# Scalings of K and Q features on GpSimd instead of VectorE, and another order of work, in a linear-attention and gated-MLP block

## Chip, cores and metric

The kernel runs on one core of one Trainium2 chip, in one launch. The metric is the device time of that launch in microseconds (us), the median of several runs; lower is better. A profiled execution gives the times of single instructions.

## What is computed

S = 2048 tokens of width D = 640, one batch, bfloat16. A linear attention with 32 heads of 20 channels is followed by a bilinear MLP with 1536 hidden channels. Cut from the reference:

```
h  = x + A(layernorm(x));  out = h + B(layernorm(h))
A: q, k, v = split(x @ wqkv)                     # 32 heads x 20
   phi(u)  = concat(softmax(u @ w_phi), softmax(-(u @ w_phi)))   # 40 features per head
   kv = sum_s phi(k)_s v_s^T ;  z = sum_s phi(k)_s
   o  = (phi(q) @ kv) / (phi(q) . z + 1e-6) ;  A = o @ wo
B: ((x @ w_gate) * (x @ w_up)) @ w_down
```

## The kernel before

The tokens are 16 tiles of 128 (number t below). Every step is a named operation with an engine, what it reads and writes, and slots in small pools of buffers. The names, with the engine that runs them and the line where they are recorded:

- **Start.** x0 to x14, wk, wv, wq, w5 and the other w are loads by DMA, most of them issued by SyncE (SP). warm are matmuls on zeros. WT transposes the K weights on TensorE and F1, F0 fold w_phi into the K and Q weights; WTe and Fe copy the results out of PSUM.
- **Layernorm.** L1s, L1a (VectorE statistics), L1l, L1e (ScalarE: the reciprocal root by logarithm and exponential), L1n (line 440, a 128x1 product on GpSimd or VectorE) and xn (the normalised tile, VectorE or ScalarE, line 446); xt transposes it into xnT by DMA, or on TensorE for tiles 0 and 1.
- **K and V.** V and K are projections, ten matmuls of 320 columns each; in tiles 0 and 1 each is cut in five parts. Ve copies V out of PSUM (line 510). Kx (two instructions, exp of +u and -u) writes the K features ek, Ks sums each head's 20 on VectorE (line 495), Kr and Ke form the reciprocal on ScalarE, and **Kn** multiplies the features by it (line 515, a tensor_tensor of 128x1280). KV (line 523) adds the tile's kv and z in PSUM. KVe copies the sums out once all 16 are there.
- **Q.** Q, Qx, Qs (line 553), Qr go the same way; **Qb** (line 560) subtracts the two logarithms of a head, Qe takes the exponential, and **Qn** (line 567, tensor_tensor of 128x660) scales the second half of the features. qT transposes them by DMA.
- **Attention output.** N (line 585) multiplies by kv, dd, rd and o divide, oT is a DMA transpose, O (line 612) the output projection, h adds the residual.
- **MLP.** hc centres the tile (ScalarE, or VectorE), hT transposes it by DMA, L2q, L2v (line 633), L2r form the second layernorm's scale; U is a gate or up projection (line 655), g and u form the product, D the down projection (line 674), y scales and adds, w stores.

Tokens of the MLP go in five blocks of 2, 4, 4, 4 and 2 tiles (U0 to U4). PSUM has eight banks; a projection holds two.

The order is neither that of the code nor decided on the chip. PLAN, a table at the top of the file, holds for each operation a due time, the number of the engine chosen from a short list, and the buffer slots. Each engine's program is its operations sorted by due time, and an engine runs its program strictly in order. An operation that waits for a semaphore holds everything behind it on its engine; SP's transposes and loads stand in one such queue. The due times serve for sorting only. The lines that read the table (lines 172 and 173), and the choice that Kn has (lines 515 and 519):

```
k, a, o.slots = PLAN.get(name, (key, 0, ()))
o.eng, o.occ, o.lat = o.alts[a]
...
G.op("pool", "Kn%d" % t, lambda e, eng, ek=ek, sr=sr: e.tensor_tensor(
...
    pool_c(1280), LP, [ek, sr], [ek], kk, alts=[("dve", dve_c(1280), LD)])
```

"pool" is GpSimd, "dve" VectorE; without a number in the table the first of the list is taken. All of this comes before the attention output: KV14 and KV15 need Kn14 and Kn15, and no N can run before KVe0 and KVe1.

Of the kernel before, what the change touches and what calls it, by code (L numbers as in the profile page):

```python
# [49 lines left out]
gl0:0.78 gla2:0.942 gla3:1.084 glb3:1.313 gla1:1.452 gla0:1.594 glb2:1.736 zero:0.91 w5:0.78 Ph1:2.585 x0:0.78 L1s0:3.188 warm0:1.239 warm1:1.665 id0:2.977  # L50
id1:3.216 warm2:2.091 warm3:2.517 x1:1.26 warm4:2.943 warm5:3.369 warm6:3.795 L1a0:4.098 wk0:1.74:1 eps:3.459 L1l0:4.331 L1s1:4.207 L1a1:5.117 warm7:4.221
warm8:4.647::0 warm9:5.077 L1e0:4.657 xn0:5.226::0 L1l1:5.35 L1e1:5.676 xn1:5.914::1 WT0:5.292::1 WTe0:5.912 warm10:5.709 warm11:5.924 warm12:6.139 xt0:6.354::0
xt1:6.633::2 xte0:6.832 glb0:3.49 gla4:3.628 xte1:7.415 x3:2.22:1 L1s3:6.426 L1a3:7.336 wk1:2.7 WT1:6.912::3 WTe1:7.532 L1l3:8 L1e3:8.325 glb1:3.771 Ph0:3.999
wk3:3.18 glb4:4.593 Ph2:4.822 F1_0:7.329::4 Fe1_0:8.418:1 wk4:3.66:1 WT4:7.648::6 WT3:8.065::7 wk2:4.14:1 WT2:8.482::1 WTe2:9.101 ekz:5.415 F1_1:8.899::2
Fe1_1:9.687 WTe4:8.268:1 F1_4:9.218::4 WTe3:8.684 F1_3:9.537::6 F1_2:9.863::0 x2:4.62 L1s2:9.092 K0_0:10.447::2 L1a2:10.002 Fe1_4:10.271:1 K0_1:10.719
L1n3:8.605 xn3:10.111::2 Fe1_3:10.623:1 K1_0:11.031::4 K1_1:11.303 wv0:5.1:1 V1_0:11.573::6 Fe1_2:10.854:1 K1_2:11.845 x4:5.58 L1s4:11.364 L1a4:12.274
K1_3:12.116 K1_4:12.386 K0_2:12.658 K0_3:12.928 x6:6.06 L1s7:12.383 L1s5:13.169 L1l2:11.438 L1e2:11.764 L1n2:12.044 xn2:12.347:1:3 wv4:6.54:1 Kx1_0:13.152::0
Kx1_1:13.736 L1a5:14.079 L1l4:14.319 L1e4:14.646 L1s6:14.188 x14:7.02 wv1:7.5 V1_1:13.2 L1n5:14.976:1 xn5:15.13::0 wv2:7.98:1 V1_2:13.47 L1a6:15.642 K0_4:13.742
Kx0_0:14.739::1 Kx0_1:15.322 L1n4:15.751:1 xn4:15.906:1:1 V0_0:14.012::0 V0_1:14.284 va1:12.268 L1a7:15.796 L1l6:16.712 wv3:8.46 V1_3:14.555 V0_2:14.825
V0_3:15.097 xt3:10.736 x8:12.046 Ks0:16.058::0 V0_4:15.367 V3:15.639::4 Ve3:17.195::0 V1_4:16.994 Ve1:17.779::1 wqt1:12.527 Kr0:18.363 Ke0:18.654 Kn0:18.988  # L60
K3:17.265::2 Kx3_0:18.822::2 x10:13.836 phz:21.3 xt2:14.316 K2:18.622::4 L1s9:17.451 Kx3_1:19.405 L1a9:18.361 xt5:15.755 Ks1:18.471::1 Kr1:19.989 Ke1:20.28
L1s8:19.863 L1a8:20.773 L1e6:20.427 L1n6:20.883:1 L1n7:20.927:1 xt4:17.064 xn7:21.081::2 Kx2_0:20.52::3 wqt4:18.375 wg4:19.684 L1l8:21.104 L1e8:21.43
L1n9:21.668:1 wqt2:20.165 V2:19.977::6 K5:21.334::2 Ve2:21.534::2 Ve0:22.117::3 K4:22.689::6 Kx5_0:22.89::4 Sz:22.017 Kx5_1:23.474 L1s10:21.712 L1n8:22.195
xt7:21.706 Kx2_1:24.058 KV0:24.046::0,1 Ks3:22.5::2 Kr3:24.642 Ke3:24.933 mk0:22.419 V4:24.378::2 Ve4:25.934::4 V5:25.735::4 xn6:23.892::3 L1a10:24.404
x12:23.017 Ks2:24.794::3 xn9:26.186::0 Kx4_0:26.518::1 xn8:26.698::1 Ve5:27.291:1:5 Kx4_1:27.102 Kn1:22.48 KV1:27.09 Ks4:28.021::0 Kn3:25.267 L1s11:29.415
Ks5:30.201::1 L1a11:31.595 Kr2:27.686 Ke2:27.977 K7:27.424::2 wqt3:23.497 Kx7_0:28.98::0 Kx7_1:29.564 Kn2:28.311 V7:28.779::6 Ve7:30.335::6 L1s15:31.703
L1a15:32.614 L1s14:32.722 L1a14:33.633 wqt0:24.806 F0_0:30.136::4 Fe0_0:30.919 Kr5:31.713 L1l10:31.86 L1e10:32.185 L1n11:32.465 xt6:26.116 V6:30.454::2
xt9:27.427 Ve6:32.279::7 xt8:28.736 F0_3:31.811::6 Fe0_3:32.862 wo2:30.047 KV2:32.13 K6:32.462::4 Kr4:33.447 Ke4:33.737 Kn4:34.072 F0_2:33.819::2 Ke5:33.883
Kx6_0:34.029::3 Kx6_1:34.614 xn11:33.742::2 xt11:34.367 Fe0_2:35.197 L1s12:34.254 wu1:35.676 KV3:34.138 K9:34.471::6 wg0:36.157 Kn5:36.385 Kx9_0:36.026::2
Kx9_1:36.611 V8:35.827::4 L1s13:35.041 L1a13:35.95 Ve8:37.383::3 L1a12:36.059 L1l12:37.967 L1e12:38.292 Ks7:36.169::2 rqz:38.697 L1n15:38.734 F0_4:37.182::2  # L70
Fe0_4:38.386 L1n12:38.959 L1n10:37.562:1 xn10:38.969:1:3 Ks9:37.606::3 Kr9:39.775 KV4:37.502 F0_1:37.834::6 Fe0_1:38.999:1 K8:38.154::4 Kx8_0:39.92::1 KV5:39.51
Kx8_1:40.505 K11:39.843::2 Kx11_0:41.398::4 Kx11_1:41.983 Q0_0:41.199::6 Q0_1:41.471 xt10:39.913 Q3:41.742::4 xn15:39.739::0 xt15:41.222 wo0:42.532
Ks6:40.252::0 Kr6:42.566 Ke6:42.858 Q0_2:43.109 Q0_3:43.382 Q0_4:43.654 wg2:43.013 L1n13:41.645:1 xn13:41.798::1 xt13:43.492 L1n14:39.182 Kn6:43.191 Ke9:43.004
Ks8:42.31::1 wg1:44.803 Q1_0:43.925::2 Qx3_0:43.307::0 Qx3_1:43.917 Kr7:44.528 wu0:45.282 Ke7:44.819 Kn7:45.505 Qs3:44.712 Kr8:44.965 Q1_1:44.197
Qx0_0:45.111::1 Qx0_1:45.721 Q1_2:44.469 Q1_3:44.742 Q1_4:45.014 Qx1_0:46.331::2 Qx1_1:46.941 mk1:47.818 Ke8:47.55 Kn8:48.088 xn14:46.148::2 Q9:45.285::4
Qx9_0:47.697::3 Qx9_1:48.306 V10:46.653::6 Ve10:48.916::1 KV6:48.008 K10:48.342::2 Kn9:50.401 Kx10_0:49.898::3 Qs0:46.66 Kx10_1:50.481 KV7:49.697 xn12:48.094::3
K13:50.031::4 Kx13_0:51.587::0 Qr3:52.17::0 Kx13_1:52.316 Q2:51.386::6 Qx2_0:52.952::4 xt12:48.719 xt14:50.029 mk2:52.714 Ks11:48.606::0 Qr0:53.562::1
Qb3:52.984 Qb0:53.906 Qx2_1:53.708 Qs9:49.999 Qr9:54.318::2 Qb9:54.661 Ks10:51.434::2 Kr10:54.464 wd2:51.34 Ke10:54.755 Qe3:54.901 V9:52.754::2 Ve9:55.02::2
Qn3:55.208 Ks13:53.053::1 wd3:51.819 Q5:54.109::4 Qx5_0:55.675::5 V12:55.477::6 Kr13:56.285 Kr11:56.431 qT3:56.542::0 Qe9:56.577 Qs1:54.446 KV8:56.833
KV9:57.166 Ke13:56.696 Qs2:55.88 Qr1:56.842::3 Qe0:56.987 Qn0:57.316:1 Qb1:57.185 Ke11:57.106 Qe1:57.461 Qn1:57.767 qT1:59.102::1 Qn9:59.032 Qr2:57.58::0  # L80
Qb2:58.166:1 Qx5_1:57.725 Qe2:58.38 Qn2:60.297 K12:57.498::2 Kx12_0:59.054::1 Kx12_1:59.639 Ve12:58.266:1:0 K15:58.855::4 Kx15_0:60.41::2 Kx15_1:60.995
wu3:61.578:1 Kn10:58.996:1 Q4:60.211::6 Qx4_0:62.059::0 Qx4_1:62.669 Q10:61.578::2 Ks15:61.73::3 KV10:62.944 Kr15:63.279 Ke15:63.569 Ks12:63.123::2 Kn13:61.562
Qs4:64.516 Qx10_0:63.715::2 Qx10_1:64.326 Qs10:65.951 qT2:61.633::2 K14:63.278::4 qT9:63.123::3 wd0:66.028 Kx14_0:64.936::3 Kx14_1:65.519 qT0:66.508::4
Kr12:66.103 Ke12:66.394 Qr4:66.54::1 Qb4:67.386:1 Ks14:67.487::1 Qs5:68.879 wu2:68.209 V11:64.633::6 Kn15:63.904 Ve11:66.686::4 Q13:65.99::2 Qe4:67.602
Qn4:70.314:1 qT4:71.293::5 wu4:72.782 Qx13_0:67.721::4 Qx13_1:68.331 Qs13:71.165 V13:67.356::4 Kn11:66.216 Kr14:68.999 Ke14:69.29 V14:68.713::6 Ve14:70.269::5
Ve13:70.853::7 Kn12:68.529 Qr10:71.436::3 Q6:70.069::2 Qx6_0:71.633::3 Qx6_1:72.243 Qs6:73.038 Kn14:70.843 V15:71.436::6 Ve15:72.992::6 KV11:72.791 KV12:73.124
KV13:73.457 KV14:73.79 KV15:74.124 Q7:74.457::4 KVe0:74.654 Qr5:73.576::2 Qb5:73.919 Qe5:74.195 Qn5:74.501 Qr13:74.314::0 Qx7_0:76.022::1 Qb13:75.766
Qe13:76.632 wg3:73.263 Qn13:76.939 Qx7_1:76.751 KVe1:75.243 N0:75.823::2 qT5:76.347::4 dd0:76.355::0 rd0:76.57 N2:76.156::6 dd2:76.853::1 o0:76.972::0
oT0:77.9::0 Q11:76.49::0 Qx11_0:78.055::0 Qx11_1:78.665 rd2:77.784 o2:78.186::1 N1:77.856::4 dd1:78.998::0 rd1:79.213 o1:79.615::2 qT13:79.21::2 Q8:78.189::2
N3:79.556::6 Qx8_0:80.558::5 Qx8_1:81.168 dd3:80.427::0 Qs7:80.532 Qr7:82.085::1 Qb7:82.43 rd3:81.968 o3:82.371::0 oT1:80.7::1 N9:79.889::0 dd9:83.181::0  # L90
Q14:80.572::4 O0:81.984::2 Qe7:82.704 Q12:83.343::6 Qx14_0:83.419::4 Qx14_1:84.029 h0:83.541 rd9:84.341 oT2:82.01::2 o9:84.745::2 Qb10:82.629 Qe10:84.639
N4:84.71::2 dd4:85.555::0 rd4:85.77 O1:85.043::4 o4:86.174::1 Qn7:83.011 h1:86.984 O2:86.4::0 h2:87.957 N5:87.758::2 dd5:88.757::0 rd5:88.972 oT3:83.32::3
O3:88.091::4 Qr6:84.758::2 hc0:84.904::0 o5:89.376::0 qT7:84.629::1 hc1:87.919::1 hc2:88.892::3 h3:90.186 Q15:89.45::0 Qs14:90.987 oT9:86.12::0 O9:90.817::2
# [822 lines left out]
```

## Time and profile before

| what | before |
|---|---|
| median of 3 runs | 276.71 us (275.79 to 277.2) |
| profiled execution, whole | 273.92 us |
| its span on the core | 272.2 us |
| TensorE busy in the span | 265.4 us |
| VectorE / ScalarE / GpSimd busy | 169.1 / 125.6 / 66.4 us |
| Kn on GpSimd: 15, mean | 2399 ns |
| Kn on VectorE: 1 | 1908 ns |
| Qn on GpSimd: 12, mean | 1428 ns |
| Qn on VectorE: 4, mean | 1250 ns |
| granted TensorE clock | 1.00 |

Lines of the profile name engines PE (TensorE matmuls), PEld (its weight loads), DVE (VectorE), ACT (ScalarE), POOL (GpSimd) and SPq (SyncE's queue, which issues DMAs). L515 is line 515 of the kernel. In the page's second part each digit is the busy share, in tenths, of one of 40 equal slices of the span, 6.8 us each. In the chain, columns are start, length and what ran; in the timeline they are start, length, engine, line, operation, tile written and tiles read, count, and in brackets the engine's idle time before it with what ended it. Operations can be told apart in the timeline since each engine runs its program in the written order.

### The profile page before, as it was taken

The numbers are of one execution on the slowest core, as the hardware profiler recorded it, in microseconds if no ns is written. First come the engines' busy times: TensorE is split into PE (matmuls) and PEld (weight loads), VectorE is DVE, ScalarE is ACT, GpSimd is POOL, SyncE is SP. The second block draws the span as 40 slices with busy tenths as digits, with TensorE's granted clock in tenths as the row PEclk, the third lists the DMA queues.
The fourth block names the chain that finished last, engine by engine and source line by source line (L and its number), as shares of the span: only waits on it lengthen the run. The fifth ranks groups of instructions, "written<-read, shape, count | busy, mean of one in ns | idle before, by whom it ended". The sixth has DMA issues, their size and how long they took to land.

```text
span 272.2 us, 5184 instructions
## 1 busy us (share of the span) xinstructions
PE 265.4 (97%) x2096; PEld 176.5 (65%) x2096; DVE 169.1 (62%) x304; ACT 125.6 (46%) x309; POOL 66.4 (24%) x88
## 2 busy tenths in 40 slices
...
DVE  5999998999989979587835435313332511434332
ACT  4998899989846565632332223530031210404000
POOL 6229476879954033001100000000000000000000
...
## 3 DMA queue, kind: packets, MB, share of 16 engines
...
q14 instruction: 8, 0.07, 0.1%
...
## 4 chain that ended last, share of the span: by engine, by line
PE 85%; POOL 7%; ACT 3%; DVE 3%; DMA 2%; issue 0%; DVEq 0%
PE ps L655 37%; PE ps L674 19%; PE ps L479 16%; PE ps L612 7%; POOL ek L515 4%; POOL ph L567 2%; DMA Wp<-o 2%; PE ps L585 1%; DVE o L602 1%; PE ps L364 1%; PE ps L523 1%; PE ps L408 1%; ACT ph L548 1%; DVE sm L599 1%; ACT ek L491 0%; ACT xnT L247 0%
## 5 line engine op out<-in xcount | busy, mean ns | idle before, releaser
L655 PE MATMUL ps<-xnT,Wgu 128*128 128x512 bf16 (+1 forms) x600 | 108.0, 336 | 0.0
L655 PEld LDWEIGHTS ps<-xnT,Wgu 128*128 128x128 bf16 x600 | 58.0, 98 | 43.0 <-DVE ev L663 0.2
L660 ACT ACTIVATE gt<-ps 128x512 bf16<-128x512 f32 (+1 forms) x60 | 29.6, 509 | 98.0 <-PE ps L655 86.5
L479 PE MATMUL ps<-Wp,xnT 128*128 128x320 bf16 (+1 forms) x480 | 68.5, 299 | 0.2 <-DVE o L602 0.2
L663 DVE TENSOR_TENSOR ev<-ps,gt 128x512 bf16<-128x512 f32 (+1 forms) x60 | 33.2, 579 | 43.4 <-ACT gt L660 20.8
L479 PEld LDWEIGHTS ps<-Wp,xnT 128*128 128x128 bf16 x480 | 45.2, 97 | 18.6 <-DVE o L602 0.6
L674 PE MATMUL ps<-Wd,ev 128*128 128x320 bf16 (+2 forms) x396 | 53.8, 295 | 0.0
L674 PEld LDWEIGHTS ps<-Wd,ev 128*128 128x128 bf16 x396 | 38.1, 98 | 15.6
L686 DVE SCALAR_TENSOR_TENSOR Wp<-ps,rs,x_all 128x640 bf16<-128x640 f32 (+3 forms) x18 | 14.6, 810 | 39.7 <-PE ps L674 39.5
L515 POOL TENSOR_TENSOR ek<-ek,SR 128x1280 bf16<-128x1280 bf16 x15 | 35.7, 2399 | 11.9 <-ACT SR L500 11.9
L633 POOL TENSOR_SCALAR ln<-mv 128x1 f32<-128x1 f32 x10 | 1.9, 190 | 111.1 <-ACT ek L629 110.8
L612 PE MATMUL ps<-Wo,Wp 128*128 128x320 bf16 x160 | 24.2, 299 | 0.9 <-DMA Wp<-o 0.9
L553 DVE TENSOR_REDUCE S<-ph 128x66 f32<-128x1320 bf16 x16 | 24.1, 1519 | 1.0 <-ACT ph L550 1.0
L495 DVE TENSOR_REDUCE SR<-ek 128x64 f32<-128x1280 bf16 x16 | 23.5, 1472 | 0.4 <-ACT ek L491 0.2
L548 ACT ACTIVATE ph<-ps 128x600 bf16<-128x600 f32 x32 | 21.2, 678 | 3.8 <-PE ps L479 2.3
L491 ACT ACTIVATE ek<-ps 128x640 bf16<-128x640 f32 x32 | 20.7, 700 | 1.5 <-PE ps L479 1.3
L612 PEld LDWEIGHTS ps<-Wo,Wp 128*128 128x128 bf16 x160 | 15.4, 98 | 7.0 <-DMA Wp<-o 1.2
L567 POOL TENSOR_TENSOR ph<-ph,RQ 128x660 bf16<-128x660 bf16 x12 | 17.1, 1428 | 10.9 <-ACT RQ L563 10.7
L618 DVE SCALAR_TENSOR_TENSOR x_all<-ps,x_all 128x640 bf16<-128x640 f32 x16 | 13.1, 821 | 7.7 <-PE ps L612 7.4
L629 ACT ACTIVATE ek<-x_all,mv 128x640 bf16<-128x640 bf16 x16 | 13.1, 820 | 4.7 <-DVE x_all L618 4.7
L602 DVE TENSOR_TENSOR o<-ps,sm 128x720 bf16<-128x720 f32 x16 | 14.5, 906 | 0.8
L560 POOL TENSOR_TENSOR RQ<-RQ 128x32 f32<-128x32 f32 x14 | 3.3, 238 | 29.4 <-ACT RQ L556 29.4
...
## 6 DMA issues: line engine op xcount, KB each, us to landing
...
```

Of the source, the lines that this page charges most:

```text
L479: ins = e.matmul(pb(b, hb)[:, 0:n1 - n0], lhsT=T["xnT"][:, NC - 1 - c, P * t:P * (t + 1)], rhs=T["Wp"][:, POS[kind], c, n0:n1], start=(c = ...
L491: G.op("act", "%sx%d_%d" % (nm, t, s), lambda e, s=s, b=b, ek=ek: e.activation(out=T["ek"][:, ek.slots[0], 0:2 * D].rearrange("p (b h s f) ...
L495: G.op("dve", "%ss%d" % (nm, t), lambda e, ek=ek, sr=sr: e.tensor_reduce(out=T["SR"][:, sr.slots[0], 0, :], in_=T["ek"][:, ek.slots[0], 0: ...
L515: G.op("pool", "Kn%d" % t, lambda e, eng, ek=ek, sr=sr: e.tensor_tensor(out=T["ek"][:, ek.slots[0], 0:2 * D].rearrange("p (h f) -> p h f", ...
L548: e.activation(out=v[:, 0:10].rearrange("p (b g) j f -> p b g j f", b=2), in_=pp(b, 0, 300).rearrange("p b (g j f) -> p b g j f", j=3, f=D ...
L553: G.op("dve", "Qs%d" % t, lambda e, t=t, ph=ph: e.tensor_reduce(out=T["S"][:, t, 0:66].rearrange("p (g k) -> p g k", k=6), in_=pv(ph).rear ...
L567: return e.tensor_tensor(out=v, in0=v, in1=T["RQ"][:, rq.slots[0], 1, 0:33].rearrange("p (g j) -> p g j", j=3).unsqueeze(3).to_broadcast([ ...
L612: ins = e.matmul(pb(b, hb)[:, 0:320], lhsT=T["oT"][:, oT.slots[0], c, :], rhs=T["Wo"][:, c, 320 * hb:320 * (hb + 1)], start=(c == 0), stop ...
L655: ins = e.matmul(pb(b)[:, 0:n], lhsT=T["Wgu"][:, gu, c, P * ft:P * (ft + 1)], rhs=T["xnT"][:, NC - 1 - c, o0:o0 + n], start=(c == 0), stop ...
L660: G.op("act", "g%d_%d" % (bi, ft), lambda e, pg=pg, gt=gt, n=n: e.activation(out=T["gt"][:, gt.slots[0], 0:n], in_=pb(pg)[:, 0:n], func=AF ...
L663: o_ = G.op("dve", "u%d_%d" % (bi, ft), lambda e, pu=pu, gt=gt, hh=hh, ft=ft, n=n: e.tensor_tensor(out=T["hh"][:, hh.slots[0], ft, 0:n], i ...
L674: ins = e.matmul(pb(b, hb)[:, 0:w], lhsT=T["hh"][:, hh.slots[0], ft, P * tt:P * (tt + 1)], rhs=T["Wd"][:, ft, c0 + w * hb:c0 + w * (hb + 1 ...
```

## The change

Only PLAN changes: due times, engine choices and slots, hence each engine's order. No function, operation or shape does. 49 of 1025 operations change engine:

| operations | from | to |
|---|---|---|
| Kn10; Qn0, Qn4, Qn11, Qn12; Qb2, Qb4 | VectorE | GpSimd |
| Qb12 | GpSimd | VectorE |
| L1n4, 5, 6, 7, 9, 10, 13; L2v3, 4, 10, 11, 12 | VectorE | GpSimd |
| L1n3, 8, 11, 15; L2v0, 1, 5, 15 | GpSimd | VectorE |
| Ve4, 11, 13, 14; WTe0; xn2, xn10; hc6, hc7 | ScalarE | VectorE |
| Ve5, Ve12; Fe1_3, Fe0_1; xn6; hc10, 11, 14, 15 | VectorE | ScalarE |
| x1 (issue) | SP | ScalarE |
| w5, wu3 (issue) | ScalarE | SP |

A few entries of the diff (name:due time:engine number:slots):

```diff
-Qb2:58.166:1 Qx5_1:57.725 Qe2:58.38 Qn2:60.297 K12:57.498::2 Kx12_0:59.054::1 Kx12_1:59.639 Ve12:58.266:1:0
...
-wu3:61.578:1 Kn10:58.996:1 Q4:60.211::6
...
+Qb9:54.175 Qe9:54.853 Q2:52.852::2 Kn10:54.431 V9:54.219::4 Qs5:55.515
...
+Qb2:61.609 Ks12:61.829::2
```

The orders that result, where they differ most. GpSimd, from Kn6 to Kn14:

```
before: Kn6 Kn7 mk1 Kn8 Kn9 mk2 Qb3 Qb0 Qb9 Qn3 Qb1 Qn1 Qn9 Qn2 Kn13 Kn15 Kn11 Kn12 Kn14
after:  Kn6 L1n14 L1n13 mk2 L1n12 Kn7 Kn8 Kn9 Kn11 Qb1 Qb0 Qn0 Qn1 Qb9 Kn10 Kn13 Qb3 Qb5 Qn3
        Qb2 Qn2 Kn15 Qn5 Qn9 Kn12 Kn14
```

TensorE, the first projections, and from N7 to N15 (U0_4_1 is block 0, column tile 4, 1 for up):

```
before: F1_1 F1_4 F1_3 F1_2 K0_0 K0_1 K1_0 K1_1 V1_0 K1_2 ...
after:  F1_0 F1_2 F1_4 F1_1 V1_0 V1_1 V1_2 F1_3 V1_3 K1_0 K1_1 ...
before: N7 U0_10_0 U0_0_1 U0_1_1 U0_0_0 U0_5_0 O4 U0_1_0 N10 U0_2_0 U0_3_1 U0_4_1 U0_3_0 U0_2_1 U0_9_0 N6
        U0_4_0 U0_6_1 U0_10_1 U0_5_1 O5 U0_6_0 U0_8_0 O7 O6 U0_7_0 U0_9_1 O10 N15
after:  N7 U0_10_0 U0_2_0 U0_0_0 U0_1_1 U0_9_0 U0_0_1 O4 N10 U0_1_0 U0_2_1 O5 U0_5_0 N6 U0_7_1 U0_4_0
        U0_3_1 U0_3_0 U0_5_1 U0_4_1 U0_8_0 U0_7_0 O7 U0_6_1 U0_6_0 O10 U0_11_0 O6 U0_11_1 N15
```

SP's queue at the start and around oT6:

```
before: x0 x1 wk0 x3 wk1 wk3 wk4 wk2 x2 wv0 x4 x6 wv4 ...   qT6 oT7 hT3 hT2 oT10 wd1 oT6 qT15 hT5 hT4
after:  w5 wk0 x0 wk4 x3 wk3 wk2 wk1 wv0 x4 wv1 wv2 wv3 ... wd3 qT6 oT7 hT3 oT10 hT5 hT2 oT6 qT15 hT4
```

More of the change, by code (lines that the diff above doesn't have):

```diff
@@ L49 @@
 for _t in """
[L50 to L93, printed above, removed]
@@ L102 @@
-Qe11:107.364 oT6:102.826::1 hc4:107.483::1 h7:107.275 qT15:104.136::5 O6:107.075::4 h6:108.632 hT5:106.647 Qn11:109.433:1 hc7:108.21::2 U0_7_0:108.433::1
-L2q0:108.927 g0_8:109.787::2 U0_9_1:108.979::0 g0_7:110.061::3 O10:109.525::6 h10:111.082 N15:110.883::4 hT4:108.338 L2v5:107.55 dd15:111.882::0 rd15:112.097
-o15:112.501::2 U0_7_1:111.216::2 qT14:109.648::4 u0_7:113.311 U0_8_1:111.762::1 u0_8:113.642 hc6:110.335::3 u0_9:113.973 U0_11_0:112.308::6 qT11:111.138::1
-hT7:113.319 oT15:114.629::2 U1_0_0:112.854::7 N13:113.933::4 dd13:114.464::0 rd13:114.679 o13:115.082::1 U1_1_0:114.266::2 g0_11:113.763::3 U1_2_0:115.345::1
@@ L106 @@
-Qs12:115.893 g1_2:116.622::2 U1_5_0:116.424::6 g1_1:117.109::1 L2v2:117.328:1 N14:117.503::4 U1_3_0:117.836::0 Qr12:117.596::2 dd14:118.034::0 rd14:118.249
-o14:118.653::0 U1_9_0:118.915::1 u0_10:119.463 U0_11_1:119.995::2 u0_11:120.739 Qb12:117.94 Qe12:118.215 Qn12:121.07:1 O15:120.54::4 L2q7:118.334 L2v7:119.382
-L2v1:119.549 hT6:115.939 L2v0:119.718 L2v9:119.885 h15:122.097 hc15:123.031:1:0 g1_9:120.192::0 Qs8:123.484 Qr8:125.037::0 Qb8:125.382 Qe8:125.656
-U1_0_1:121.898::3 D0_0:122.978::1 oT14:119.579::3 O14:126.237::4 hc10:124.919:1:1 L2r2:125.373 L2r0:125.442 y0_0:126.436::0 g1_0:125.775::3 hT15:123.606
@@ new lines @@
+L1a1:4.098 L1l1:4.331 wk0:1.26:1 va1:1.708 warm4:2.943 warm5:3.369 warm6:3.795 warm7:4.221 x0:1.74 L1s0:4.207 L1a0:5.117 warm8:4.647::0 warm9:5.077 warm10:5.292
+L1e1:4.657 warm11:5.507 xn1:5.226::0 gla2:2.538 L1l0:5.35 L1e0:5.676 xn0:5.914::1 gla4:2.68 warm12:5.722 id0:2.822 id1:3.061 xt1:5.937::0 wk4:2.22:1 x3:2.7:1
+WT0:6.216::1 WTe0:6.835:1 xt0:6.633::2 wk3:3.18 xte1:6.415 xte0:7.111 L1s3:7.244 wk2:3.66:1 gla1:3.304 wk1:4.14 WT4:6.912::3 WTe4:8.03:1 WT2:7.407::4 L1a3:8.438
+WTe2:8.027 L1l3:8.671 WT3:7.824::5 WTe3:8.547 wv0:4.62:1 WT1:8.241::6 WTe1:8.956 L1e3:8.998 glb4:3.446 Ph2:3.675 L1n3:9.364:1 x4:5.1 xn3:9.648::2 L1s4:10.159
@@ new lines @@
+L1s5:10.947 L1a4:11.733 glb1:4.269 Ph0:4.497 L1a5:11.857 phz:5.091 glb2:5.808 Ph1:6.036 F1_0:8.658::0 Fe1_0:9.175:1 F1_2:8.977::2 wv1:5.58 F1_4:9.296::4
+Fe1_4:9.813:1 ekz:6.428 F1_1:9.615::6 Fe1_1:10.397 Fe1_2:10.981:1 V1_0:9.936::0 rqz:6.662 wv2:6.06:1 V1_1:10.207 V1_2:10.478 F1_3:10.749::4 Fe1_3:11.565
+wv3:6.54 V1_3:11.068 K1_0:11.339::6 K1_1:11.61 x2:7.02 L1s2:11.966 L1a2:12.876 L1l4:12.149 L1e4:12.475 L1n5:12.755 xn5:13.057::3 K0_0:11.881::2 K0_1:12.152
+K0_2:12.423 K0_3:12.694 K0_4:12.965 x6:7.5 L1s7:13.569 L1l2:13.108 L1e2:13.434 L1n2:13.714 xn2:14.356::0 Kx0_0:13.527::0 Kx0_1:14.111 K1_2:13.236 K1_3:13.507
@@ new lines @@
+Kn2:28.623 Kx7_1:31.104 L1n11:32.745:1 x14:22.502 L1s14:32.92 xt6:22.982 V6:29.901::0 wqt3:24.292 Ve6:31.688::7 KV2:31.257 KV3:31.59 L1n10:31.291 Kr4:32.272
+Ke4:32.563 wqt4:25.602 wqt1:26.912 F0_2:31.923::2 Fe0_2:32.709 L1a14:33.83 F0_3:32.242::4 Fe0_3:33.293 L1s15:33.939 K6:32.561::0 Kx6_0:34.117::3 Kx6_1:34.701
+F0_0:33.917::2 wu3:28.222 xn11:34.726::2 Kn5:31.515 Fe0_0:35.285 xt9:29.326 K9:34.236::4 Kx9_0:35.869::2 Kx9_1:36.453 xt8:30.678 V8:35.592::0 Ve8:37.148::1
+L1a12:35.238 Kn4:33.828 wg0:31.988 L1s13:35.347 Ks6:36.134::2 Kr6:37.732 Ke6:38.023 Kn6:38.357 L1a15:37.527 L1a13:37.636 KV4:36.948 L1l12:38.169 xt11:35.351
@@ new lines @@
+L1e12:38.495 L1n14:40.67 Ks7:37.745::0 L1n13:40.894 mk2:41.118 L1n12:41.389 KV5:37.281 F0_4:37.614::2 Fe0_4:38.588 wu1:36.661 F0_1:37.933::4 Fe0_1:39.172
+K8:38.252::0 Kx8_0:39.808::0 Kx8_1:40.392 xn10:39.138::3 Kr7:40.976 Ke7:41.267 Kn7:41.612 K11:39.608::2 Q3:40.964::4 Kx11_0:41.413::4 Kx11_1:41.997
+Q1_0:42.331::0 xt10:39.763 wo2:41.073 Ks9:39.65::3 Q1_1:42.603 Ks8:41.128::1 Q1_2:42.875 Q1_3:43.147 Q1_4:43.419 Q0_0:43.691::2 Qx3_0:42.581::0 Kr8:43.191
+Ke8:43.482 Q0_1:43.963 Q0_2:44.235 Qx3_1:43.628 Kn8:43.925 wu0:41.553 xn12:42.521::0 Q0_3:44.507 Q0_4:44.779 Qx1_0:44.238::1 xn13:43.033::1 Ks11:43.545::2
@@ new lines @@
+Qs9:51.252 Qr9:53.66::2 Kr10:53.806 Ke10:54.097 Qs3:52.687 Qx5_1:54.243 Ks13:54.122::1 Qb9:54.175 Qe9:54.853 Q2:52.852::2 Kn10:54.431 V9:54.219::4 Qs5:55.515
+Ve9:55.775::4 Kr13:56.359 Qx2_0:56.505::5 Ke13:57.115 Kn13:57.449 Qx2_1:57.261 Qr3:57.871::3 V12:55.575::0 Ve12:58.017::3 K15:56.931::4 Kx15_0:58.601::0
+Kx15_1:59.185 Qs2:58.056 Qb3:59.762 KV9:58.287 KV10:58.62 Ks15:59.921::3 Qr5:59.769::1 Qb5:60.113 wu2:56.651 Qe3:60.037 Qn3:60.344 K12:58.953::2 Qr2:60.156::0
+Q4:60.309::0 Kx12_0:60.509::2 Kx12_1:61.093 Qe5:61.677 V14:61.676::4 Qb2:61.609 Ks12:61.829::2 qT3:61.679::2 wg1:63.169 Ve14:63.232:1:6 Qe2:61.884 Qn2:62.191
@@ new lines @@
+Kr15:62.003 Ke15:62.294 Kn15:63.456 Kr12:63.341 Qx4_0:63.487::2 Qx4_1:64.097 Qs4:64.892 Q10:63.032::2 Qx10_0:64.707::1 qT2:63.649::3 Qx10_1:65.317 Qs10:66.327
+Qn5:65.769 wo0:65.349 Qr4:66.445::3 K14:64.399::4 V13:65.755::0 Ve13:67.762:1:2 Ke12:66.591 Kx14_0:66.737::3 Kx14_1:67.321 Ks14:68.493::0 Q13:67.111::2
+Qx13_0:68.676::0 Qx13_1:69.286 V11:68.478::4 Ve11:70.034:1:7 Q6:69.834::0 KV11:71.201 Kr14:70.005 Ke14:70.296 Qs13:70.765 Qn9:67.034 qT9:68.369::4 Kn12:68.299
+Qx6_0:71.399::5 Qx6_1:72.009 Qs6:72.804 V15:71.534::2 qT5:69.859::5 KV12:72.89 KV13:73.223 Ve15:73.09::5 Kn14:70.63 KV14:73.556 KV15:73.889 KVe0:74.42
@@ new lines @@
+KVe1:75.009 Q7:74.222::4 Qb4:72.943 Qe4:73.674 Qn4:73.981 N0:75.589::0 dd0:76.12::0 rd0:76.335 wg4:72.039 N1:75.922::2 Qr13:73.793::0 dd1:76.625::1
+Qx7_0:75.787::3 Q11:76.255::6 Qb13:75.246 qT4:76.113::0 o0:76.749::0 Qe13:76.397 Qn13:76.704 N2:77.705::0 oT0:77.676::0 rd1:77.56 Qx7_1:76.516 Qx11_0:77.82::4
+Qx11_1:78.43 Q8:78.038::4 Qx8_0:80.323::2 qT13:78.986::1 o1:77.974::1 N3:79.405::2 Q14:79.738::6 dd2:78.785::0 rd2:79 oT1:80.476::1 Qx8_1:80.933 o2:79.414::2
+oT2:81.786::2 N9:81.105::0 dd3:80.225::0 O0:81.75::4 Qs7:80.331 Qr7:81.884::1 rd3:81.766 o3:82.18::0 oT3:83.107::3 h0:83.307 dd9:84.127::0 rd9:84.342
```

104 lines of the change are left out of this document (64 added, 40 removed).

## The prediction

> **What bounds the kernel now.** I read the page's busy shares first, then its slices, the chain that ended last, and the timeline around the two longest stops of TensorE.
>
> ```profile
> span 272.2 us, 5184 instructions
> ...
> PE 265.4 (97%) x2096; PEld 176.5 (65%) x2096; DVE 169.1 (62%) x304; ACT 125.6 (46%) x309; POOL 66.4 (24%) x88
> ...
> DVE  5999998999989979587835435313332511434332
> ACT  4998899989846565632332223530031210404000
> POOL 6229476879954033001100000000000000000000
> ```
>
> TensorE is busy for 265.4 of 272.2 us. Both kernels run the same matmuls, so whatever an order can win lies in the other 6.8 us: about 1.3 us of start, 2.7 us behind the last matmul, and 2.9 us of stops between. Up to slice 11 (75 us) VectorE is as full as TensorE and ScalarE nearly so; GpSimd fills up at the end of that stretch. There a late feature can stop TensorE. After 112 us the chain is TensorE alone. The chain of waits names two places:
>
> ```profile
> 58.02 5.31 POOL ph L567 x3
> 63.33 12.24 POOL ek L515 x5
> 75.56 0.05 issue
> 75.61 0.85 PE ps L523 x22
> ...
> 105.50 4.59 DMA Wp<-o
> 110.09 0.05 issue
> 110.14 1.53 PE ps L612 x10
> ```
>
> First place: KV14 waits for Kn14, the end of 17.5 us of unbroken GpSimd work. The timeline by engine shows why that work was long:
>
> ```profile
> 58.02 5.31 POOL L567 TENSOR_TENSOR ph<-ph,RQ 128x660 bf16<-128x660 bf16 x3 [0.34 <-ACT RQ L563]
> ...
> 60.26 1.91 DVE L515 TENSOR_TENSOR ek<-ek,SR 128x1280 bf16<-128x1280 bf16 x1
> ...
> 70.86 2.48 DVE L567 TENSOR_TENSOR ph<-ph,RQ 128x660 bf16<-128x660 bf16 x1
> ...
> 75.61 0.85 PE L523 MATMUL ps<-ev,ek 128*128 128x63 bf16 x22 [1.39 <-POOL ek L515]
> ...
> 110.14 0.31 PE L612 MATMUL ps<-Wo,Wp 128*128 128x320 bf16 x1 [0.88 <-DMA Wp<-o]
> ```
>
> A Qn alone takes 1.30 us on GpSimd (ten of the twelve), a Kn 2.36. The three Qn from 58.02 took 5.31 instead of 3.9, and Kn14 took 2.95, while VectorE ran its own Kn10 and Qn4. Qn4 took 2.48 on VectorE where the three Qn that meet no GpSimd work take 0.84; a Qb there took 1.29 against 0.18. So the two engines' two-input operations waited for each other: GpSimd lost 1.2 (Qn2), 0.2 (Qn1) and 0.6 (Kn14), 2.0 us ahead of KV14. The wait of 1.39 is less than that. Second place: O6 waits 0.88 us for oT6, issued at 105.50 just behind the 480 KB weight load wd1 and landing 4.6 us later, where the median for that transpose is 2.7.
>
> **The scalings moved.** Kn10, Qn0, Qn4, Qn11, Qn12, Qb2 and Qb4 go from VectorE to GpSimd, Qb12 the other way. VectorE sheds 1.9 + 0.8 + 2.5 + 0.8 + 0.8 + 1.3 + 0.2 = 8.3 us, 6.7 of it ahead of KVe0. GpSimd gains 2.36 + 4 x 1.30 + 2 x 0.24 - 0.24 = 7.8 us. Only Qb12 is left on VectorE with two SBUF inputs, at about 123 us when GpSimd is nearly empty, so I price the mutual blocking at nothing: 2.0 us come back to GpSimd. The order also puts Qn5 and Qb5 ahead of Kn14, so ahead of KV14 GpSimd has Kn10, Qn0, Qn5, Qb2 and Qb5 more and the 2.0 less: 2.36 + 2 x 1.30 + 2 x 0.24 - 2.0 = 3.4 us; some L1n add 0.8.
>
> [...]
>
> **Does GpSimd still finish before TensorE needs KV14?** Ahead of KV14 both orders give TensorE the same projections, folds and KV steps, so it arrives at 74.22 us plus what the start slips. GpSimd from Kn7 to Kn14 has nine Kn, six Qn and six Qb: 21.2 + 7.8 + 1.4 = 30.4, less 0.04 of overlap at each step = 29.7 us. When can Kn7 begin? Now GpSimd idles 3.73 us before Kn6 (43.30), since Ks6 stands at 40.23 on VectorE and Kr6 behind the Kx8 and Kx11 pairs on ScalarE. In the new order Ks6 stands ahead of Ks7 and Kr6 directly behind Ve8, which ended at 38.17. That lets Kn6 start near 38.9, and Kn7 (Ke7 behind Kx8, near 42.1) near 42.3 instead of 45.6. Walked step by step with the rows' durations, waits for Kr13 (0.7, behind Ve9), Qe5 and Qe2 (0.9 in all) and others leave 1.9 us of idle time on GpSimd: 42.3 + 29.7 + 1.9 = 73.9, ahead of TensorE by 0.3 to 0.8. The stop of 1.39 goes: **-1.4**. If the cover is gone, each us of lateness costs one us.
>
> **The other moves ahead of KVe0.** VectorE takes Ve4, Ve11, Ve13, Ve14 (0.8 each), xn2, xn10 and WTe0, and gives up Ve5, Ve12, Fe1_3, Fe0_1 and xn6. Of its own L1n it hands over seven and takes four. With the scalings it has about 6 us less to do (11.9 given up, 5.6 taken), ScalarE about 1.6 less. Ve14, Ve13 and Ve11 free PSUM pairs: by the walk they end 0.3 to 1.3 us before their next users. All three sit behind a 1.4 us reduction; lying tight, they are priced at zero but keep up to 0.5 for the range.
>
> **Start.** SP issues w5 and wk0 ahead of x0, which goes at 1.72 us instead of 0.80; x1 goes by ScalarE's queue. The first normalised tiles come some 0.3 us later. On VectorE the copies WTe0, WTe4, WTe3, WTe1 follow with L1s3 between, so the last ends near 9.8 and F1_1 follows; V1_0 to V1_3 then stand ahead of K1_0, and each needs its wv load (issued about 4.5 to 6.4, median 4.9 to landing, so 9.4 to 11.3). When V1_3 has ended (11.7) the old order is 0.3 us further. I take **+0.4**; ends -0.2 (the old stop of 0.3 before F1_4 goes, nothing new) and +1.2 (the last wv late).
>
> **77 to 112 us.** oT, hT and qT transposes pass SP's queue one by one, 1.3 us each. The new order puts O5 early and O10 and three U ahead of O6; oT6 is issued behind hT2, near 105.2, and TensorE asks for O6 near 110.5. Even 4.6 us to landing is in time: **-0.9**. wd1 goes behind qT11, wd0 behind oT15, with nothing urgent next. But wd3 now goes just ahead of qT6 (near 95.1): with 4 to 5.9 us to landing N6 would wait 0 to 0.6. Q12 now takes the banks of N3 and so waits for o3 near 84.2, 0.4 us, where now Q14 waits 0.23 for o1. O5, U0_4_0 and O15 follow their releasers by 0.1 to 0.3. Together **+0.5** (bounds 0 and 1.5).
>
> **112 us to the end.** The L2v swaps (0.14 against 0.19), hc6, hc7, hc10, hc11, hc14, hc15 (0.54 on VectorE, 0.83 on ScalarE) lie on engines under half full, beside a TensorE that never stops there. hT13 and hT12, last before U3_8_0, have some 4 us to spare. Zero; a new stop could cost up to 0.5. The last six D groups keep their length.
>
> **Sum.** -1.4 + 0.4 - 0.9 + 0.5 = -1.4. The profiled execution took 273.92 us (span 272.2 and 1.7 around it), so 272.5. The median shown, 276.71, lies 1.0% above that execution, with runs of 275.79 to 277.2; I put the difference on the median: **275.3 us**.
>
> **Rivals.**
> 1. Only one stop goes. GpSimd is in time, but the 0.9 us comes back as waits behind wd3 and o3, or O6 is late again. For it: SP's queue stays as full. Then -0.5: 276.2.
> 2. Slower: GpSimd becomes the bound. The point is Kn7's start plus idle time: 29.7 us must fit before about 74.6. If Ke7 stays as late as now (Kn7 at 45.6) and the idle is the 2.6 us that GpSimd has today from 53 to 58, Kn14 ends at 77.9: a wait of 3.3 in place of 1.39, +1.9. With the start at +0.4 and the second place unchanged, 279.0. It decides once start delay and idle time exceed 2.6 us together against my 1.9. For: more work there. Against: VectorE, which paced Ks, has 6 us less.
> 3. The start slips by its upper end and only KV14's stop is won, with the tight PSUM handovers taking 1.0: 1.2 - 1.4 + 1.0 = +0.8, 277.5.
> That the change does less than said is excluded by the order listing: Kn and Qn stand on GpSimd all 32 times.
>
> **How the numbers follow.** A measurement of this kernel can tell about 0.5%, 1.4 us, from no change, and my forecast lies on that edge. Forecast 0.47 (0.40 beyond the edge: with the start at -0.2 or the 77 us stretch at 0 it gives 274.7), rival 1 0.24 (0.05 beyond, since runs spread 0.3%), rival 2 0.18, rival 3 0.11 (0.07 past the upper edge). Faster 0.45, same 0.07 + 0.19 + 0.04 = 0.30, slower 0.25. Winning all 2.9 us gives 273.8; below stands little. The upper end takes in most of rival 2: 273.6 to 278.8.
>
> **What would show it.** Right: KV14 directly behind KV13; every Kn near 2.36 and every Qn near 1.30 on GpSimd; Kn7 starting near 42 and Kn14 ending before 74.7; O6 without a wait on its transpose; TensorE busy near 265 in a span near 270.8. Wrong: a wait of L523 or L479 on GpSimd's ek over 1 us (rival 2), first projections past 11.0 us (rival 3), N6 or O waiting on scratch or Wp (rival 1).

## The result: 1.0% faster, and the profile after

The changed kernel took 273.22 us (median of 4 runs, 272.96 to 274.77) where the kernel before took 276.4 (4 runs, 275.79 to 277.2): a ratio of 0.9895, 95% interval 0.9849 to 0.9941. A second comparison on another occasion gave 273.46 (273.35 to 273.73) against 276.11, ratio 0.9902 (0.9879 to 0.9926). The gain is 2.7 to 3.2 us; 1.4 was forecast, and the time lies under the range of 273.6 to 278.8.

The profiled execution took 273.25 us (span 271.5), so on the profiles alone (273.92 before) the gain would be 0.7. This contradiction is the main subject of what follows. The page of the changed kernel:

```profile
span 271.5 us, 5179 instructions
...
PE 266.3 (98%) x2096; PEld 178.0 (66%) x2096; DVE 160.3 (59%) x294; ACT 125.4 (46%) x309; POOL 72.7 (27%) x98
...
DVE  4898999887988899774555643314324221414342
ACT  3799799988766475373135322106312230021100
POOL 8028769989952232204000000000000000000000
...
L515 POOL TENSOR_TENSOR ek<-ek,SR 128x1280 bf16<-128x1280 bf16 x16 | 37.5, 2356 | 4.4 <-ACT SR L500 4.4
L567 POOL TENSOR_TENSOR ph<-ph,RQ 128x660 bf16<-128x660 bf16 x16 | 20.8, 1306 | 11.9 <-ACT RQ L563 11.9
```

VectorE lost 8.8 us and GpSimd gained 6.3. All 16 Kn (L515) now take 2.36 us on average, all 16 Qn (L567) 1.31: nothing is blocked any more. The chain of waits of the changed kernel, around the two places where TensorE used to stop:

```profile
73.76 1.36 PE ps L479 x10
75.13 1.35 PE ps L523 x44
76.48 1.38 PE ps L479 x10
...
88.38 4.72 DMA Wp<-o
...
107.73 1.36 PE ps L612 x10
110.18 1.36 PE ps L612 x10
112.08 1.36 PE ps L612 x10
```

KV12 to KV15 (L523, 44 matmuls) run as one piece, where the old chain came from GpSimd; and no DMA stands ahead of the O steps (L612) near 110 us. What the chain has new is a transpose at 88.38 (oT9, for O9). The timeline by engine gives the margins, and the start:

```profile
6.80 0.71 PE L459 MATMUL ps<-ident,xn 128*128 128x128 bf16 x5 [0.88 <-DVE xn L450]
...
8.38 2.26 PE L389 MATMUL ps<-ident,ev 128*128 128x128 bf16 x20
...
67.88 2.57 POOL L567 TENSOR_TENSOR ph<-ph,RQ 128x660 bf16<-128x660 bf16 x2
70.40 4.71 POOL L515 TENSOR_TENSOR ek<-ek,SR 128x1280 bf16<-128x1280 bf16 x2
...
74.97 1.52 PE L523 MATMUL ps<-ev,ek 128*128 128x63 bf16 x44
...
111.92 1.52 PE L612 MATMUL ps<-Wo,Wp 128*128 128x320 bf16 x10
```

GpSimd ends Kn14 at 75.11, TensorE reaches KV14 at 75.65. But TensorE is late itself: xt1 waited 0.88 us for its first tile, and the 20 transposes behind it took 2.26 us. The old order would have been at KV14 at 74.22 us without its stop (75.61 less 1.39); the new one is 1.43 us behind that. GpSimd's work shifts with TensorE's: in a second profile of the changed kernel (below) KV14 came at 74.81 and Kn14 had ended at 74.27, again 0.54 us ahead.

### The profile page after: what moved, and what is told of

It reads as the page before. It is cut to its first block, busy times and chain, and to the rows that moved or that the text cites. A ratio compares the mean times of both kernels' runs of the same rounds, so it can differ in the third digit from the quotient of the medians.

```text
span 271.5 us, 5179 instructions
## 1 busy us (share of the span) xinstructions
PE 266.3 (98%) x2096; PEld 178.0 (66%) x2096; DVE 160.3 (59%) x294; ACT 125.4 (46%) x309; POOL 72.7 (27%) x98
## 3 DMA queue, kind: packets, MB, share of 16 engines
HBM read 11.00 MB, written 2.62 MB: 50 GB/s over the span
## 4 chain that ended last, share of the span: by engine, by line
PE 92%; DVE 3%; DMA 3%; SPq 0%; issue 0%; DVEq 0%
PE ps L655 38%; PE ps L479 22%; PE ps L674 19%; PE ps L612 7%; PE ps L523 2%; DMA Wp<-o 2%; DVE o L602 1%; PE ps L585 1%; DMA x_all<-in_A_x_dram 1%; PE ps L408 1%; PE ps L389 1%; DVE S L553 1%; DVE sm L599 0%; PE ps L459 0%; SPq L281 0%
## 5 line engine op out<-in xcount | busy, mean ns | idle before, releaser
L515 POOL TENSOR_TENSOR ek<-ek,SR 128x1280 bf16<-128x1280 bf16 x16 | 37.5, 2356 | 4.4 <-ACT SR L500 4.4
L612 PE MATMUL ps<-Wo,Wp 128*128 128x320 bf16 x160 | 24.0, 299 | 0.1
L567 POOL TENSOR_TENSOR ph<-ph,RQ 128x660 bf16<-128x660 bf16 x16 | 20.8, 1306 | 11.9 <-ACT RQ L563 11.9
L612 PEld LDWEIGHTS ps<-Wo,Wp 128*128 128x128 bf16 x160 | 15.4, 98 | 6.4 <-DMA Wp<-o 0.5
L627 ACT ACTIVATE xn<-x_all,mv 128x640 bf16<-128x640 bf16 x11 | 9.0, 827 | 9.6 <-DVE x_all L618 9.6
```

Source lines behind the costliest of these rows:

```text
L567: return e.tensor_tensor(out=v, in0=v, in1=T["RQ"][:, rq.slots[0], 1, 0:33].rearrange("p (g j) -> p g j", j=3).unsqueeze(3).to_broadcast([ ...
L612: ins = e.matmul(pb(b, hb)[:, 0:320], lhsT=T["oT"][:, oT.slots[0], c, :], rhs=T["Wo"][:, c, 320 * hb:320 * (hb + 1)], start=(c == 0), stop ...
```

## Experiments

Letters stand for theories: L, the kernel before was profiled in an unusually quick execution (N: its median was high by chance); Q, what the order gives GpSimd decides, not who runs the scalings (S in that run: taking two-input work off VectorE pays in any order); D, what differs between executions is the landing of DMAs, and the changed kernel depends on it less; G, the gap at the start costs what it shows; W, wd1's place ahead of oT6 costs more than its first profile showed; in the last runs S, SyncE's transposes bind from 77 to 95 us; T, TensorE is full there. The "before" beside each group was 276.6 (first four), 276.11 (next four) and 276.09 us (last three).

### The kernel before once more

No edit.

> The kernel before, once more, to settle how far its profiled execution (273.92 us, span 272.2) stands for it, since its median was 276.4. Theory L (the medians differ by more than the traces because the profiled execution of before was a lucky one): most runs near 276.4 us with spans near 274.6, and a new profile shows 2 to 2.5 us more than the first, at one or two named places. Theory N (the median was high by chance of the chip): runs near 274.

Measured: 276.0 us (274.53 to 278.22), ratio 0.9974 (0.9946 to 1.0002). Its profiled execution took 275.76, span 274.0. Here is the second stop in its timeline:

```profile
108.64 1.52 PE L612 MATMUL ps<-Wo,Wp 128*128 128x320 bf16 x10
111.99 1.53 PE L612 MATMUL ps<-Wo,Wp 128*128 128x320 bf16 x10 [1.83 <-DMA Wp<-o]
```

O6 waited 1.83 us, not the 0.88 of the first profile. On SyncE's queue hT3 was issued 1.08 us later than in the first profile, hT3 and hT2 together took 3.67 us to issue instead of 2.91, and oT10 behind them 1.73 instead of 1.20; oT6 went out at 107.87 instead of 105.50 and landed 4.07 later. The wait at KV14 was 1.39 again, to the hundredth, although KV14 came 0.54 later (76.15). So of the two stops one is fixed and the other depends on the execution. The first profile had also been an unusually quick execution: 273.92 us, where the quickest run of this kernel in any later comparison took 274.53. The last matmul ended at 271.33 here and at 269.48 in the first profile; of these 1.85 us, 0.54 had come ahead of KV14, 0.36 between KV14 and O6, and 0.95 are O6's longer wait. Theory L holds in the main, but half of what it explains is not at one place.

### The seven scalings alone, in the old order

```diff
+for _n in "Kn10 Qn0 Qn4 Qn11 Qn12 Qb2 Qb4".split():
+    PLAN[_n] = (PLAN[_n][0], 0) + PLAN[_n][2:]      # 0 GpSimd, in the old plan
```

> The kernel before with only Kn10, Qn0, Qn4, Qn11, Qn12, Qb2, Qb4 moved to GpSimd, at the places that the old order gives them. [...]

Measured: 279.79 us (279.23 to 280.56), ratio 1.0109 (1.0078 to 1.0140): 3.2 us slower. Its timeline on TensorE, then its time by stage:

```profile
69.75 1.66 PE L481 MATMUL ps<-Wp,xnT 128*128 128x320 bf16 x11
74.62 4.57 PE L481 MATMUL ps<-Wp,xnT 128*128 128x300 bf16 x20 [3.21 <-ACT ph L552]
79.02 1.86 PE L525 MATMUL ps<-ev,ek 128*128 128x63 bf16 x55
```

```profile
64.00:74.60 10.60, 7.36 (x62) 4.92 (x59) 8.26 (x7) 6.73 (x22) 10.60 (x7) 1.00 0.87 184
74.60:78.20 3.60, 3.58 (x14) 2.06 (x15) 1.52 (x1) 2.37 (x8) 3.60 (x3) 0.53 0.38 108
```

GpSimd (the fifth busy time of each row) is busy for all of 64 to 78.2, and Kn14 ends at 78.89 instead of 75.55. TensorE first stops 3.21 us ahead of Q6, behind features that wait for GpSimd, and then runs at a granted clock of 0.53 (the column after POOL). This is the second rival's mechanism, in the old order: moved alone, the scalings make GpSimd the bound. Theory Q had the time (2 to 3.3 us longer) and the end of Kn14 (78 to 79); the stop came at Q6 and not, as it said, at KV14. Theory S, which had the time 0.4 to 1.4 us shorter, falls.

### The new order with the scalings on VectorE

```diff
+for _n in "Kn10 Qn0 Qn4 Qn11 Qn12 Qb2 Qb4".split():
+    PLAN[_n] = (PLAN[_n][0], 1) + PLAN[_n][2:]      # 1 VectorE, in the new plan
```

> The changed kernel with only Kn10, Qn0, Qn4, Qn11, Qn12, Qb2, Qb4 back on VectorE, at the places of the new order. If the scalings carry the gain: Qn2, Kn13 or Kn14 on GpSimd longer than 2.5 us again, Ks and Qs on VectorE 2 to 4 us later, KV14 or a Q projection stops TensorE for 1 to 3 us, time 1 to 3 us longer. If the new order alone carries it: within 0.5 us of the changed kernel, since GpSimd then has 8 us less to do.

Measured: 274.76 us (274.16 to 275.27), ratio 0.9926 (0.9897 to 0.9955). By the ratios (0.9895 and 0.9902 for the changed kernel) it is 0.7 to 0.9 us slower, by the medians 1.3 to 1.5; the intervals of the ratios overlap, so the size is rough. KV14 does not wait: Kn14 ends at 74.55, after 3.46 us of idle time on GpSimd. Its start is like that of the changed kernel's second profile: KV14 comes at 74.82 here and at 74.81 there. The price appears behind it, in the timeline of VectorE and TensorE:

```profile
75.60 0.18 DVE L562 TENSOR_TENSOR RQ<-RQ 128x32 f32<-128x32 f32 x1
76.08 0.84 DVE L569 TENSOR_TENSOR ph<-ph,RQ 128x660 bf16<-128x660 bf16 x1 [0.30 <-ACT RQ L565]
76.85 0.91 DVE L532 TENSOR_TENSOR KVm<-ps,mask 128x504 bf16<-128x504 f32 x2
...
77.82 0.85 PE L587 MATMUL ps<-KVm,scratch 128*128 128x63 bf16 x22 [0.79 <-DVE KVm L532]
```

Qb4 and Qn4 stand ahead of KVe0 (L532) on VectorE, and N0 waits 0.79 us for KVe0: it comes at 77.82, where that second profile has 76.86, and the last matmul ends at 269.69 instead of 268.96. So the order by itself ends the stop at KV14; the scalings on GpSimd keep VectorE free for what comes right after it.

### Five more matmuls ahead of the first tile

```diff
-NFILL = 5
+NFILL = 10
+for _k in range(13, 18):
+    PLAN["warm%d" % _k] = (5.9 + 0.001 * _k, 0, ())
```

> The changed kernel with five more 256-column matmuls on zeros between the last filler and xt1 (5.92 to about 7.0 us), so that TensorE has no gap of 0.88 us there. Theory G (the gap delayed the grant of the full clock from 6.06 to 10.42 us, and the transposes took 0.53 us for five instead of 0.27): grant near 6 to 8 us, V1_0 near 10.7 instead of 11.84, time 0.8 to 1.3 us shorter. Rival (the start waits for loads and copies, not for the clock): V1_0 where it was or 0.2 later, time the same within 0.3.

Measured: 272.81 us (272.39 to 274.01), ratio 0.9862 (0.9828 to 0.9895); again beside the last two kernels below, as the control that its expectation describes:

> The changed order with five further zero matmuls ahead of xt1, again, beside the two kernels above and on their chip. It had 272.81 (272.39 to 274.01) beside a before of 276.6. If the five matmuls are worth 0.4 to 0.6 us, it is 0.4 to 0.6 under the changed order without them (here: the one with qT7 behind oT9, less what that brings); if the earlier start is lost before 95 us, the two are within 0.3.

273.08 us (272.17 to 273.36), ratio 0.9891 (0.9874 to 0.9908). Lower than the changed kernel's ratio both times, by 0.33% and 0.11%, with intervals that overlap: a gain is not shown. In the first of the two profiles the edit did not do what it was meant to: xt1 still waited 1.30 us, since x0 landed at 5.55 instead of 5.12. In the second that gap was gone. V1_0 came at 11.09 in the first of the two profiles instead of 11.84, but Q12, O9, N6 and U1_5_0 then waited 0.23, 0.21, 0.38 and 0.14 us, and O6 started at 111.92, as it did without the five matmuls.

### The changed kernel once more, and x0 first in SyncE's queue

The first has no edit; the second one line:

```diff
+PLAN["x0"] = (0.7,) + PLAN["x0"][1:]
```

> The changed kernel once more beside the next three, for a second profile. Theory D (the time that differs between executions of the same kernel is DMA landing time, and the changed kernel depends on it less): runs within 1 us of each other around 273.2, no wait on a transpose over 0.5 us from 77 to 112 us. Rival (the first profile was a lucky one as well): spans 1 us or more above 271.5, with a new stop.

> The changed kernel with x0 first in SP's queue, as in the kernel before, so that L1s0 need not wait for it. Theory G (the idle gap ahead of xt1, and the half clock behind it, are the price of the new start): xt1 near 6.0 instead of 6.8, full clock granted by 8 us, V1_0 near 10.2 to 10.8 instead of 11.84, time 0.8 to 1.4 us shorter than the changed kernel. Rival (copies and weights set the start): V1_0 at most 0.3 earlier, time the same within 0.4.

Measured: 273.46 us (273.35 to 273.73), ratio 0.9902 (0.9879 to 0.9926) without the edit, and 273.99 (273.12 to 275.01), ratio 0.9919 (0.9891 to 0.9947) with it. With it x0 landed at 3.69 instead of 5.12, but xt1 came at 6.64, not near 6.0. V1_0 started at 10.72, as theory G had it, and the time did not follow. Theory G falls, and the profile of the kernel without the edit shows why:

```profile
6.66 0.45 PE L459 MATMUL ps<-ident,xn 128*128 128x128 bf16 x5 [1.01 <-DVE xn L450]
...
7.68 1.45 PE L389 MATMUL ps<-ident,ev 128*128 128x128 bf16 x20
...
92.88 1.53 PE L612 MATMUL ps<-Wo,Wp 128*128 128x320 bf16 x10 [0.65 <-DMA Wp<-o]
94.25 0.50 PE L585 MATMUL ps<-KVm,scratch 128*128 128x63 bf16 x11
94.74 2.45 PE L655 MATMUL ps<-xnT,Wgu 128*128 128x256 bf16 x21
```

In this execution of the same kernel the transposes were quicker (1.45 us for 20, not 2.26), V1_0 started 1.32 us sooner (10.52) and KV14 0.84 sooner (74.81). Yet O9 waited 0.65 us for oT9, U0_10_0 started at 94.74 against 94.86, and the last matmul ended at 268.96 against 268.80. The earlier start was lost on the way. SyncE's queue shows where, first in the first profile, then in this one (qT4, then oT0):

```profile
78.28 1.53 SPq L572 DMA_TRANSPOSE scratch<-ph  x1
79.86 1.32 SPq L606 DMA_TRANSPOSE Wp<-o  x1
```

```profile
77.45 2.34 SPq L572 DMA_TRANSPOSE scratch<-ph  x1
79.83 1.28 SPq L606 DMA_TRANSPOSE Wp<-o  x1
```

qT4 was issued 0.83 us earlier and took 0.81 longer to issue, so oT0 went out at the same time. With x0 first qT4 took 2.48. With the five matmuls it took 1.39, and hT0, behind oT9, 2.32 instead of 1.28, so the lead was lost there. From the issue of oT0 to that of oT9 pass 8.50 to 8.63 us in all four profiles, transposes issued one right behind the other, so nothing lost is won back. Why one transpose takes a microsecond longer in some executions is not shown. Theory D is right on the spread (0.38 us over six runs) and not on the waits (0.65 for oT9, where it had at most 0.5).

### wd1's place, both ways

```diff
+PLAN["wd1"] = (108.5,) + PLAN["wd1"][1:]      # old plan: behind oT6, qT15, hT5 and hT4
```
```diff
+PLAN["wd1"] = (104.3,) + PLAN["wd1"][1:]      # new plan: just ahead of oT6
```

> The kernel before with only the load wd1 (480 KB) moved from ahead of oT6 to behind hT4 in SP's queue. Theory W (the load delays oT6): oT6 lands within 2.7 us and 0.6 us earlier in issue, O6 waits 0 to 0.4 instead of 0.9 to 1.8 us, time 0.9 to 1.6 us shorter. Rival (oT6 is late because SP issues it late, behind slow transposes): O6 still waits 0.7 us or more, time at most 0.7 shorter.

> The changed kernel with only wd1 moved to just ahead of oT6, where the old order has it. Theory W: oT6 issued 0.6 later and landing 4 to 4.6 instead of 2.6 us after its issue, at 112 or later, O6 waits 0 to 1 us, time 0.2 to 1.0 us longer than the changed kernel. Rival (the new order asks for O6 late enough in any case): the same within 0.3 us.

Measured: moving wd1 back in the old order gives 274.37 us (273.51 to 275.19), ratio 0.9934 (0.9908 to 0.9959), a gain of 1.7 us by one entry. Putting it ahead of oT6 in the new order gives 274.81 (273.42 to 276.99), ratio 0.9955 (0.9928 to 0.9982), 1.35 us over the changed kernel beside it. In the timeline of the old order with wd1 moved:

```profile
108.97 1.25 PE L656 MATMUL ps<-xnT,Wgu 128*128 128x256 bf16 x10
110.06 2.88 PE L613 MATMUL ps<-Wo,Wp 128*128 128x320 bf16 x20
```

oT6 landed 2.64 us after its issue, and O6 follows O7 without a stop (20 matmuls in one piece). This was the slowest of the six runs (275.19): it had lost 2.27 us by U0_10_0 against the first profile of before, elsewhere than at O6. The new order with wd1 ahead was profiled in its quickest execution; oT6 took 4.27 us to land and O6 still came in time, at 111.69. What its slower executions, up to 276.99, wait for was not profiled, so the 1.35 rests on the times alone.

The four kernels timed here side by side form a square: 276.11 and 274.37 us in the old order, with wd1 ahead of oT6 and behind it, 274.81 and 273.46 in the new one. wd1's place is worth 1.74 and 1.35 us, everything else in the change 1.30 and 0.91. Theory W holds in direction; both values of wd1's place lie above what it had (0.9 to 1.6 and 0.2 to 1.0).

### qT7 behind oT9

```diff
+PLAN["qT7"] = (87.0,) + PLAN["qT7"][1:]
```

> The changed order with one entry moved: qT7 (the transpose of Q7's features, first needed by N7) goes behind oT9 on SyncE's queue. In the changed kernel's run of call 2, oT9 was issued at 88.34, right behind qT7 (86.86), though o9 had ended at 87.14; it landed at 92.83 and O9 waited 0.65 for it. Theory S (the start's gain is lost at SyncE's transposes, which run one behind the other from 77 to 93 us): oT9 is issued at about 87.2 and lands near 91.5, O9 does not wait (it started 92.88, and could at 92.3), but hT1, whose place in the queue is not changed, still lands near 94.3, so that U0_10_0 starts at about 94.3 instead of 94.74: at most 0.45 us comes off, 273.0 against 273.5, within what can be told. Theory T (TensorE itself is full from 77 to 95, and the waits shown are only where its slack shows): O9's wait goes, but it shows again at N7 or U0_10_0 (qT7 lands 1.4 to 1.5 later, near 93.7; N7 stood at 94.25), and U0_10_0 stays at 94.7: 273.5.

With the five matmuls as well:

> The changed order with qT7 behind oT9, and the five further zero matmuls ahead of xt1 that gave 272.8 by themselves. Theory S: hT1 still sets U0_10_0 at about 94.3, where it was with the five matmuls alone (94.33), so nothing more comes off: 272.8, the same as the kernel beside it. Theory T: the 0.21 us that O9 waited comes off, 272.6, which can't be told from 272.8. If both changes are worth what their waits show, U0_10_0 at 94.0 and 272.4.

Measured: 273.81 us (273.57 to 275.48), ratio 0.9931 (0.9909 to 0.9953), and with the five matmuls 273.85 (273.74 to 274.08), ratio 0.9924 (0.9910 to 0.9939), where the control had 0.9891: 0.8 us slower. Both theories missed it. In the second kernel's timeline of TensorE and ScalarE:

```profile
91.87 1.52 PE L615 MATMUL ps<-Wo,Wp 128*128 128x320 bf16 x10
93.22 0.50 PE L588 MATMUL ps<-KVm,scratch 128*128 128x63 bf16 x11
95.51 1.69 PE L658 MATMUL ps<-xnT,Wgu 128*128 128x256 bf16 x14 [1.78 <-ACT ph L553]
...
92.99 0.67 ACT L551 ACTIVATE ph<-ps 128x600 bf16<-128x600 f32 x1 [3.99 <-DMA scratch<-ph]
...
95.15 0.21 ACT L553 ACTIVATE ph<-ps 128x40 bf16<-128x40 f32 x1
```

oT9 landed in 2.63 us and O9 (L615, 91.87) no longer waited, as both expected. But Qx12 on ScalarE (L551) reuses the ph buffer that qT7 empties. qT7 now landed at 92.97, Qx12_1 ended at 95.36, and U0_10_0 (L658), which takes over Q12's PSUM bank, started at 95.51 instead of the control's 94.08. The last matmul ended 0.79 later (269.41 against 268.62), the medians differ by 0.77. So what SyncE's queue does between 77 and 95 us sets the time, by a chain that the expectation did not have: transpose, feature buffer, ScalarE, PSUM, TensorE.

## Why the prediction was wrong

- **KV14, -1.4: right in mechanism and size.** The old order stopped there 1.39 us in each of three profiles, the changed one in neither of two. Kn7 started at 43.62 (42.3 was forecast, 45.6 before) and Kn14 ended at 75.11 (73.9), late by the slip of the start: in the second profile they stand at 42.79 and 74.27. The prediction walked GpSimd's work as if it did not depend on the start. The cover is 0.54 us in both profiles, within the 0.3 to 0.8 of the forecast. That the scalings belong to it is half shown: the order alone also ends the stop, at 274.76, with a cover of 0.27.
- **Mutual blocking, nothing: right.** Kn 2.36 and Qn 1.31 throughout. With the scalings back on VectorE the new order had hardly any either (Kn13 2.46 on GpSimd; Kn10 on VectorE 1.48, 1.91 before), so the move is not the only way to end it. The traces show operations that took longer (in the first profile of before Qn4 2.48 us on VectorE, where others took 0.84, and beside it Kn14 2.95 on GpSimd, where others took 2.36); that the two engines wait for each other is the author's reading of that.
- **Rival 2, GpSimd as the bound: false here, true in the old order** (279.79; that the rival said 279.0 is chance, since its sum was for the new order). Moved alone, the scalings cost 3.2 us. In the new order GpSimd starts earlier (Kn7 at 43.62 instead of 45.6) and VectorE is kept free for the work that TensorE needs next, and GpSimd is 0.54 us ahead at KV14.
- **Rivals 1 and 3: neither came.** Both stops went. The net gain of rival 1, 0.5 us, is what the profiles alone show (0.68 and 0.52, below), but not for its reason. The start was as late as rival 3 had it (1.43) in one of two profiles.
- **O6, -0.9: the mechanism was right, the size is the first half of the step that failed.** The term was sized from one wait of one execution, 0.88. A second execution waited 1.83 and the old order with the scalings moved 1.84; wd1's place alone is worth 1.74 us in the old order and 1.35 in the new one. The transpose's time to landing was reckoned with (4.6 us against 2.7), but not that another execution issues it 2.37 us later, with TensorE only 0.90 later.
- **"I put the difference on the median": the second half.** The 2.8 us between profile and median were carried along as something that both kernels have. The changed kernel has none of it (273.25 and 273.43 profiled, medians 273.22 and 273.46). Of the 1.85 us that a second profile of before shows, 0.95 is O6's wait, 0.54 lies ahead of KV14 and 0.36 between. The change takes out the first; why it loses less at the other places is open.
- **Start, +0.4: too low.** At KV14 it measured +1.43 in the first profile, beyond the upper end, and +0.59 in the second. The 0.84 between them did not reach the end: 268.80 and 268.96.
- **77 to 112 us, +0.5: too low where the start was early.** The waits were Q12 0.23 and O9 0.14 in one profile; O0 0.30, O9 0.65 and N6 0.14 in the other. What TensorE gained ahead of 77 us, SyncE's queue took back: the two terms are not independent. Together they came to 1.59 and 1.75 us, where +0.9 was forecast: the last matmul ended 0.68 and 0.52 us earlier than in the first profile of before, and the two stops there were 1.39 + 0.88 = 2.27. N6, right behind wd3 and qT6, cost 0 to 0.14.
- **112 us to the end, zero: right.** From O6 to the last matmul pass 156.88 us in both profiles of the changed kernel (111.92 to 268.80, 112.08 to 268.96).

So the forecast for the profiled execution, 272.5, was too low by 0.75 and 0.93 us (273.25 and 273.43), and the 2.8 us put on top were not there; the two errors partly cancel in 275.3. In medians the square of the wd1 runs tells it: wd1's place is worth 1.35 to 1.74 us where 0.9 stood for O6, and the rest of the change 0.91 to 1.30 where 0.5 was forecast (1.4 less 0.4 and 0.5). Both had been sized against an execution of the old order that loses less than most.
